# Sharing the first copies between two engines, and turning one tile of the last chunk, in an attention and feed-forward kernel

## The chip, the cores and the metric

The kernel runs on one core of one Trainium2 chip. The metric is the device time of one execution in microseconds (us); lower is better. A second number, the span, is what the profile of one execution covers; it is about 2 us shorter than the time. The granted clock is the share of TensorE's full speed that the profile records. Times inside an execution are counted from the start of the span.

The engines are TensorE (PE in the profile, with PEld for its weight loads), VectorE (DVE), ScalarE (ACT), GpSimd (POOL) and SyncE (SP). All of them run at once, each through its own queue, and wait for one another by semaphores.

## The reference

```python
# B, H, S, D = 4, 4, 1088, 32;  r = 8;  everything float32
def phi(x):                                   # 32 numbers of a token become 64
    a = np.einsum('rd,bhsd->bhsr', S1, x)
    b = np.einsum('rd,bhsd->bhsr', S2, x)
    return np.einsum('bhsi,bhsj->bhsij', a, b).reshape(*x.shape[:-1], r * r)
q_p, k_p = phi(q), phi(k)
kv  = np.einsum('bhsf,bhsd->bhfd', k_p, v)
z   = np.sum(k_p, axis=2)
num = np.einsum('bhsf,bhfd->bhsd', q_p, kv)
den = np.einsum('bhsf,bhf->bhs', q_p, z)[..., None] + 1e-06
x   = (num / den).transpose(0, 2, 1, 3).reshape(B * S, H * D)   # 4352 tokens of 128
h   = np.maximum(x @ w_in, 0.0)                                 # d_ff = 2048
out = h * h @ w_out
```

## The kernel before

The feed-forward part is nearly all of the work, and TensorE is its limit. A batch has 1088 tokens, cut into three chunks of 384, 384 and 320 tokens. `w_in` and `w_out` are cut into 16 blocks of the inner dimension. So there are 4 x 3 x 16 = 192 blocks; each is one product with `w_in` (`pg`), a squared ReLU (`gt`, `g2`) on ScalarE and VectorE, and one product with `w_out` that adds into `po`. The attention of the next batch is planned into the gaps of the running one. Only batch 0's attention has nothing to hide behind: this is the prologue. And only the last chunk's result has nothing behind it: this is the tail. The change touches these two ends.

What the prologue does, in order: products `kf` of the keys with `S1` and `S2`; their outer products `kp`; products of `kp` with the values (`kvp`); the queries' features through three matrices held in `sr` (`rep`, `qp`); `nd`, the numerator and denominator; then `den` and a scaling on VectorE, a transpose (`xp`, `xT`), and the first block of the feed-forward part.

```python
WARM0, WARM = 11, 4             # filler products that keep TensorE busy early on
LA = 3                          # the first product runs three blocks ahead of the second
KG = [[(0, 2), (2, 2), (4, 4), (8, 1)]] + ...   # batch 0: key tiles by group (first, count)
fpool = ctx.enter_context(tc.tile_pool(name="ffn", bufs=5))
...
# loads, one SyncE queue in program order (v's tail of 64 rows from ScalarE)
load_qk(kn[0], k, 0, 0, 512);  load_qk(kn[0], k, 0, 512, S)
load_qk(qn[0], q, 0, 0, 384)
load_v(vn[0], 0, 0);  load_v(vn[0], 0, 2, (nc.scalar, nc.scalar));  load_v(vn[0], 0, 1)
for c in range(2):
    nc.sync.dma_start(w_in32[:, 1024*c : 1024*c + 1024], moe_w_in[:, 1024*c : 1024*c + 1024])
load_qk(qn[0], q, 0, 384, S)                    # the rest of q, behind w_in
...                                             # w_out
# GpSimd's queue: 12 copies for sr, 4 for sq, the identity, and later v's tail
for h in range(H):
    for j_, o_, f_ in ((2, ...), (0, ...), (1, ...)):
        nc.gpsimd.tensor_copy(_ap(sr, 32*h, 32, 128*j_ + 32*h, ...), _ap(s_T, 0, 32, o_, f_))
for h in range(H):
    nc.gpsimd.tensor_copy(sq[32*h : 32*h + 32, 32*h : 32*h + 16], s_T[:, 0:16])
iden = cpool.tile([128, 128], F32);  make_identity(nc, iden[:])
...
# the prologue in program order (each engine takes its own in this order)
keep_warm(WARM0)
... # kf, fs for the four groups
replicated(2, 0, 128, psf, "pg")                # rep, first 128 columns
a_v(0, 0, nc.scalar)                            # v's first half, copied by ScalarE
a_kp(0, 0);  a_kv0(0);  a_kp(0, 1)
a_kv(0, 0);  a_kv(0, 1)                         # kvp, tiles 0 and 1
replicated(0, 0, 128, ...);  replicated(1, 0, 128, ...)
a_fs(0, 2);  a_fs(0, 3)
a_v(0, 1, nc.scalar)                            # v's second half
a_v(0, 2, nc.gpsimd)                            # v's tail: last in GpSimd's queue
a_kp(0, 2);  a_kp(0, 3)
for t in range(2, 9):
    a_kv(0, t)                                  # kvp, the other seven tiles
...
replicated(2, 128, 384, ...); ...               # rep, the other 256 columns
a_kvz(0)
for c in range(2):
    nc.scalar.copy(w_in[:, 1024*c : ...], w_in32[:, 1024*c : ...])   # float32 to float16
for t in range(3):
    a_nd(0, t)
...
# the main loop and the tail
for i in range(NS + 4):                         # NS = 192
    if i + LA < NS:
        ffn1(i + LA, act_square(i + LA))
    if 0 < i < NS:
        ffn2(i)                                 # w_o is stationary, g2 moves
    ...                                         # the work planned for this block
f_last(B - 1, 2)

def f_last(b, ch):                              # the three tiles of the last chunk
    po = st["po", b, ch]                        # columns are tokens
    for i in range(3):
        ...
        # copy a tile out of PSUM, turn it with TensorE, scale it by beta per token, store it
        (nc.vector.tensor_copy if i == 1 else nc.scalar.copy)(oT[:, 0:w], po[:, 128*i : 128*i + w])
        nc.tensor.transpose(op[0:w, 0:128], oT[:, 0:w], iden[:, :])
        ...                                     # scaling: VectorE for i == 1, ScalarE otherwise
        (nc.sync, nc.gpsimd, nc.scalar)[i].dma_start(
            bass.AP(out.tensor, out.offset + (b*S + 4*t) * 128,
                    [[128, w // 32], [G * 128, 32], [1, 128]]),     # 4 x 32 rows of 512 bytes
            ob[0:w, :])
```

## Time and profile before

| | before |
|---|---|
| time, median of the 3 runs given | 206.92 us (206.01 to 207.1) |
| span of the profiled run | 204.8 us, granted clock 0.997 |
| TensorE busy | 96% of the span |
| `den` starts (VectorE, end of the prologue's products) | 15.33 us |
| first feed-forward block starts | 18.16 us |
| block 8 starts | 24.41 us |
| block 176 (last before the last chunk) starts | 184.28 us |
| block 176 to the end of the span | 20.49 us |

The profile's page gives the busy times (with the share of the span and the number of instructions), the busy tenths of 40 equal slices, and the shares of the chain that ended last:

```profile
span 204.8 us, 3685 instructions
PE 196.1 (96%) x1180; PEld 124.2 (61%) x1180; DVE 143.1 (70%) x387; ACT 143.8 (70%) x322; POOL 60.4 (30%) x254
...
PE   7998999999999999999999999999999999999980
...
PE 65%; issue 21%; POOL 5%; DVE 4%; DMA 1%; ACT 1%; POOLq 0%; ACTq 0%; DVEq 0%
```

TensorE's row is nearly full from the first slices (of 5.1 us each) on, but its filler products count as busy too, so the row doesn't show the prologue's waits; the chain does. GpSimd's 5% of the chain is the surprise: an engine that is idle 70% of the time holds up the end. The chain of waits in order of time says where (start, us, what):

```profile
6.92 2.50 POOL sr L228 x3
...
9.48 0.27 POOL sq L233
...
11.43 0.24 POOL va_119 L253
...
11.71 0.42 PE kvp L321 x8
12.13 1.49 PE rep L612 x6
...
13.70 1.60 PE nd L390 x12
15.33 0.18 DVE den L406
```

Up to 11.67 us the chain is GpSimd's queue: copies for `sr`, then `sq`, the identity, and last the small copy of v's tail (`va`), for which TensorE waits.

The view by tile gives the minimum, median and maximum of those copies in ns, and the timeline (start, us, engine, line, operation, output from input, count, and in brackets the idle time before it and its releaser) shows what VectorE did meanwhile. First the tile view of `sr` in before, then the timeline of before:

```profile
L228 POOL COPY sr<-s_T x12: 201/204/1217, 5.3 to 8.2; 32x32 f32<-32x32 f32 x12
```

```profile
5.28 4.14 POOL L228 COPY sr<-s_T 32x32 f32<-32x32 f32 x12
...
7.53 2.17 DVE L301 TENSOR_TENSOR kp<-fs 128x512 f32<-128x512 f32 x3
...
11.71 0.42 PE L321 MATMUL kvp<-kp,va_119 128*33 128x64 f32 x8 [0.29 <-POOL va_119 L253]
...
18.16 0.22 PE L491 MATMUL pg<-xT,w_in 128*128 128x128 f16 x1
...
22.15 1.43 DVE L379 TENSOR_TENSOR qp<-qa,qb 128x384 f32<-128x384 f32 x2
...
22.47 1.59 POOL L248 COPY va_122<-vn 128x512 f32<-128x512 f32 x2 [0.27 <-POOL br L529]
```

The tail in the timeline of before:

```profile
197.27 0.70 PE L513 MATMUL po<-g_2684,w_o 128*128 128x320 f32 x2
198.01 0.27 ACT L570 COPY oTl<-po 128x128 f32<-128x128 f32 x1 [1.72 <-PE po L513]
...
199.09 0.71 SPq L582 DMA_DIRECT2D out_dram<-obl  x1
...
199.67 0.82 POOL L582 DMA_DIRECT2D out_dram<-obl  x1 [39.43 <-DVE obl L573]
199.94 0.64 ACTq L582 DMA_DIRECT2D out_dram<-obl  x1
```

The last feed-forward product ends at 197.97, and 6.80 us later the span ends. The trace's records of the DMA packets show the three stores landing at 201.33 (SyncE's), 202.71 (GpSimd's) and 203.38 us (ScalarE's). For a store, I call the end of its last packet the landing.

### The profile page before, as it was taken

The numbers are of one execution on the slowest core, as the hardware profiler recorded it, in microseconds if no ns is written. First come the engines' busy times: TensorE is split into PE (matmuls) and PEld (weight loads), VectorE is DVE, ScalarE is ACT, GpSimd is POOL, SyncE is SP. The second block draws the span as 40 slices with busy tenths as digits, with TensorE's granted clock in tenths as the row PEclk, the third lists the DMA queues.
The fourth block names the chain that finished last, engine by engine and source line by source line (L and its number), as shares of the span: only waits on it lengthen the run. The fifth ranks groups of instructions, "written<-read, shape, count | busy, mean of one in ns | idle before, by whom it ended". The sixth has DMA issues, their size and how long they took to land.

```text
span 204.8 us, 3685 instructions
## 1 busy us (share of the span) xinstructions
PE 196.1 (96%) x1180; PEld 124.2 (61%) x1180; DVE 143.1 (70%) x387; ACT 143.8 (70%) x322; POOL 60.4 (30%) x254
## 2 busy tenths in 40 slices
PE   7998999999999999999999999999999999999980
PEld 2774675577657655767576655767576655555640
DVE  3956977895587777976757788776757766667740
ACT  2545979858796877686887777686887765766640
POOL 4934637010426830011826420011826200000001
PEclk9999999999999999999999999999999999999998
DMA  6699401020012563020104840020112010200201
GB/s 187 160 348 239 136 20 22 2 39 0 19 20 38 158 147 77 3 38 2 40 12 71 212 126 0 3 40 0 38 20 41 2 32 0 34 7 0 38 0 32
DMA packets 31305, 12.32 MB, mean 60 GB/s; under 512 B 23399, under 2 KB 29863, under 8 KB 31287
## 3 DMA queue, kind: packets, MB, share of 16 engines
q1 hardware_dynamic: 30820, 11.97, 24.2%
q8 instruction: 9, 0.15, 0.3%
q10 hardware_dynamic: 386, 0.07, 0.2%
q14 instruction: 10, 0.07, 0.2%
q0 software_dynamic: 80, 0.07, 0.1%
HBM read 8.78 MB, written 2.23 MB: 54 GB/s over the span
## 4 chain that ended last, share of the span: by engine, by line
PE 65%; issue 21%; POOL 5%; DVE 4%; DMA 1%; ACT 1%; POOLq 0%; ACTq 0%; DVEq 0%
PE po L513 38%; PE pg L491 10%; PE nd L390 8%; PE kvp L321 3%; PE qc L364 3%; POOL br L529 2%; POOL sr L228 2%; PE kf L275 2%; DMA s_nat<-in_S_dram 1%; PE rep L612 1%; DVE qp L379 1%; ACT gt L500 1%; DVE xs L447 1%; DVE qa L374 1%; DVE mx L411 0%
## 5 line engine op out<-in xcount | busy, mean ns | idle before, releaser
L500 ACT ACTIVATE gt<-pg 128x384 f32<-128x384 f32 (+2 forms) x193 | 89.1, 464 | 39.2 <-PE pg L491 38.3
L491 PE MATMUL pg<-xT,w_in 128*128 128x384 f16 (+2 forms) x193 | 61.0, 316 | 0.5 <-ACT xT L472 0.3
L529 POOL COPY br<-beta 32x3 f32<-32x3 f32 x192 | 43.2, 225 | 50.9 <-DVE beta L454 43.3
L491 PEld LDWEIGHTS <-w_in 128*128 128x128 f16 x193 | 18.9, 98 | 19.9 <-issue 1.2
L582 POOL DMA_DIRECT2D out_dram<-obl x1 | 0.8, 816 | 39.4 <-DVE obl L573 39.4
L374 DVE STREAM_SHUFFLE qa<-qc 128x384 f32<-128x384 f32 x22 | 12.0, 590 | 0.1
L390 PEld LDWEIGHTS nd<-kvz_127,qp 128*128 128x128 f32 x72 | 10.0, 190 | 3.0 <-DVE qp L379 0.2
L379 DVE TENSOR_TENSOR qp<-qa,qb 128x384 f32<-128x384 f32 x22 | 11.7, 567 | 0.1
L390 PEld LDWEIGHTS nd<-kvz_125,qp 128*128 128x128 f32 x72 | 9.8, 190 | 3.2 <-issue 0.5
L537 DVE STREAM_TRANSPOSE oT<-po 128x384 f32<-128x384 f32 (+1 forms) x11 | 6.2, 564 | 7.9 <-PE po L513 7.9
L301 DVE TENSOR_TENSOR kp<-fs 128x1024 f32<-128x1024 f32 (+3 forms) x10 | 10.8, 1109 | 0.3 <-ACT fs L289 0.3
L390 PE MATMUL nd<-kvz_125,qp 128*128 128x132 f32 x72 | 10.2, 278 | 0.2
L390 PE MATMUL nd<-kvz_127,qp 128*128 128x132 f32 x72 | 10.3, 277 | 0.0
L350 POOL COPY kvz_127<-kvt 32x2 f32<-32x2 f32 x8 | 1.5, 186 | 25.8 <-PE pg L491 16.3
L364 PE MATMUL qc<-qT,sq 128*128 128x384 f32 x22 | 8.8, 487 | 0.0
L447 DVE TENSOR_TENSOR xs<-nd,sc 128x384 f16<-128x384 f32 (+2 forms) x13 | 6.7, 522 | 0.3
L595 PE MATMUL warm<-zero 128*128 128x512 f16 x15 | 5.7, 550 | 1.2 <-DVE zero L142 1.2
L259 DVE STREAM_TRANSPOSE qT<-qn 128x1088 f32<-128x1088 f32 (+2 forms) x5 | 5.3, 1057 | 1.9 <-DMA qn<-in_q_dram 1.9
L406 DVE TENSOR_SCALAR den<-nd 128x12 f32<-128x12 f32 x12 | 2.0, 170 | 6.3 <-PE nd L390 6.3
L369 DVE STREAM_SHUFFLE qb<-qc 128x384 f32<-128x384 f32 x11 | 6.4, 586 | 0.0
L411 DVE TENSOR_REDUCE mx<-nd 128x12 f32<-128x384 f32 x12 | 5.9, 495 | 0.0
L543 DVE TENSOR_TENSOR ob<-oT,br 128x384 f32<-128x384 f32 (+1 forms) x11 | 5.9, 534 | 0.0
(677 smaller groups left out, 413.0 us busy)
## 6 DMA issues: line engine op xcount, KB each, us to landing
vn<-in_v_dram SPq DMA_DIRECT2D x32, 64.0 KB, 3.6
kn<-in_k_dram SPq DMA_DIRECT2D x3, 544.0 KB, 7.5
qn<-in_q_dram SPq DMA_DIRECT2D x3, 544.0 KB, 3.6
out_dram<-ob SPq DMA_DIRECT2D x32, 48.0 KB, 1.8
w_in_99<-in_moe_w_in_dram SPq DMA_DIRECT2D x2, 512.0 KB
w_o<-in_moe_w_out_dram SPq DMA_DIRECT2D x2, 512.0 KB, 9.3
out_dram<-ob SPq DMA_DIRECT2D x12, 40.0 KB, 1.9
qn<-in_q_dram SPq DMA_DIRECT2D x1, 352.0 KB
```

Of the source, the lines that this page charges most:

```text
L301: nc.vector.tensor_tensor(out=_ap(kp, 0, 128, 0, [[64, 4 * n], [8, 8], [1, 8]]), in0=_ap(fs, 0, 128, 0, [[8, 4 * n], [1, 8], [0, 8]]), in1 ...
L364: nc.tensor.matmul(qc[:, 0:384], sq[:, :], qT[:, 384 * ch : 384 * ch + 384])
L369: nc.vector.stream_shuffle(in_=st[b, "qc", ch][:, 0:384], out=qb[:, :], mask=mask_b)
L374: nc.vector.stream_shuffle(in_=st[b, "qc", ch][:, 0:384], out=qa[:, :], mask=mask_a[e])
L379: nc.vector.tensor_tensor(out=qp[:, :], in0=st[b, "qa", ch, e][:, :], in1=st[b, "qb", ch][:, :], op=mult)
L390: nc.tensor.matmul(nd[:, 132 * o : 132 * o + 132], st[b, "qp", ch, e][:, 128 * o : 128 * o + 128], st[b, "kvz"][:, 132 * e : 132 * e + 132 ...
L447: nc.vector.tensor_tensor(out=_ap(st[b, "xs", ch], 0, 128, 128 * o, [[32, 4 * n], [1, 32]]), in0=_ap(st[b, "nd", ch], 0, 128, 132 * o, [[3 ...
L491: nc.tensor.matmul(pg[:, c0:c1], w_in[:, 128 * c : 128 * c + 128], st[b, "xT"][:, 384 * ch + c0 : 384 * ch + c1],)
L500: nc.scalar.activation(gt[:, c0:c1], pg[:, c0:c1], Relu)
L513: nc.tensor.matmul(st["po", b, ch][:, c0:c1], w_o[:, 128 * c : 128 * c + 128], g2s[i][1][:, c0:c1], start=(c == 0 and c0 == 0), stop=(c == ...
L529: nc.gpsimd.tensor_copy(_ap(st[b, "br"], 32 * dm, 32, 12 * ch + p0, [[4, 3]]), st[b, "beta"][32 * p0 : 32 * p0 + 32, 3 * ch : 3 * ch + 3],)
L537: nc.vector.transpose(oT[:, 0:n], st["po", b, ch][:, 0:n])
```

## The change

The intent has two halves.

- Prologue: ScalarE, idle at that time, takes four of the twelve `sr` copies, and v's tail moves ahead of `sq` and the identity in GpSimd's queue. The rest of q is loaded ahead of `w_in`. The last two groups of key tiles are cut more evenly, and four `kvp` tiles instead of two are placed early; v's second half is copied in two pieces, the `kvz` copies are dealt out anew, and two filler products go.
- Tail: in the last chunk, the first tile's 128 tokens are kept out of `po`. Their second product is turned around: `g2` is stationary and `w_o` moves, so that the tokens come out on the partitions and need no copy and no transpose. It runs four blocks behind. So the other two tiles finish first, and their copies, transposes and scalings hide under the four late products; only one scaling and one store are left at the end. GpSimd issues no store any more.

```diff
-    WARM0, WARM = 11, 4
+    WARM0, WARM = 10, 3
+    LAST = 4
-    KG = [[(0, 2), (2, 2), (4, 4), (8, 1)]] + [[(0, 4), (4, 5)]] * (B - 1)
+    KG = [[(0, 2), (2, 2), (4, 2), (6, 3)]] + [[(0, 4), (4, 5)]] * (B - 1)
     load_v(vn[0], 0, 1)
+    load_qk(qn[0], q, 0, 384, S)
     ...                                    # the two loads of w_in
-    load_qk(qn[0], q, 0, 384, S)
-    for h in range(H):
-        for j_, o_, f_ in ((2, 8, [[0, 4], [1, 8]]), (0, 0, [[1, 4], [0, 8]]), (1, 4, [[1, 4], [0, 8]])):
-            nc.gpsimd.tensor_copy(
+    for j_, o_, f_, copy in (
+        (2, 8, [[0, 4], [1, 8]], nc.gpsimd.tensor_copy),
+        (1, 4, [[1, 4], [0, 8]], nc.scalar.copy),
+        (0, 0, [[1, 4], [0, 8]], nc.gpsimd.tensor_copy),
+    ):
+        for h in range(H):
+            copy(
                 _ap(sr, 32 * h, 32, 128 * j_ + 32 * h, [[8, 4], [1, 8]]),
                 _ap(s_T, 0, 32, o_, f_),
             )
     ...                                    # sq and the identity: moved down, see below
-    a_kv(0, 0)
-    a_kv(0, 1)
+    for t in range(4):
+        a_kv(0, t)
     ...
-    a_v(0, 1, nc.scalar)
     a_v(0, 2, nc.gpsimd)
+    ...                                    # sq and the identity, now behind v's tail
+    a_v(0, 1, nc.scalar, 0, 2)
     a_kp(0, 2)
+    a_v(0, 1, nc.scalar, 2, 2)
     a_kp(0, 3)
-    for t in range(2, 9):
+    for t in range(4, 9):
         a_kv(0, t)
     ...                                    # kvp's memset earlier, kvz copies dealt out anew
-        if 0 < i < NS:
+        if 0 < i < NS - NFF:
             ffn2(i)
+        elif NS - NFF <= i < NS:           # the last chunk's 16 blocks
+            ffn2_rest(i)                   # columns 128 to 319 into po
+            if i >= NS - NFF + LAST:
+                ffn2_tile(i - LAST)
-    f_last(B - 1, 2)
+    last_copy(B - 1)                       # two copies
+    for i in range(NS - LAST, NS):
+        if i == NS - 2:
+            last_turn(B - 1)               # two transposes, two scalings, two stores
+        ffn2_tile(i)
+    last_tile(B - 1)                       # one scaling, one store (SyncE)
+    def ffn2_tile(i):
+        ...
+        nc.tensor.matmul(st["pt"][:, 0:128], g2s[i][1][:, 0:128],
+                         w_o[:, 128 * c : 128 * c + 128],
+                         start=(c == 0), stop=(c == NFF - 1))
```

Three more buffers of `g2` (eight instead of five) hold what the late tile still needs.

## The prediction

> What bounds the kernel now. The page gives a span of 204.8 us with TensorE (PE) busy 96%, clock 0.997. From about 20 to 198 us the chain of waits is PE work back to back: a feed-forward block takes 0.81 us of PE at 384 columns, 0.67 us at 320. Only the two ends can give time.
>
> Prologue before (chain of waits, timeline). GpSimd works in one queue from 4.8 to 11.67 us: 12 copies into sr (5.28 to 9.42, 0.345 us each), four into sq (0.97), the identity (0.9), last the v tail copy. PE waits for that copy (kvp at 11.71), then does the 256-column rep products to 13.62 and nd to 15.30; VectorE starts den at 15.33.
>
> Prologue after. GpSimd has 8 sr copies, then the v tail (done about 8.4). ScalarE, idle until 6.32, takes four at about 0.2 us each. Next limit: v's second half lands at about 8.3 us (DMA packets by size), ScalarE copies it after fs, and the kp products on VectorE end at about 9.5. The last kvp then ends at about 10.3 instead of 12.13; rep at 11.9 (13.62), nd at 13.4 (15.30). Gain 1.9 us (estimate from these durations). The q rest landed at about 13.2; behind the weights it would have held the earlier chain. The first w_in half now lands near 12, the second near 13.3: the casts (1.04 us each) end near 14.5, before xT (about 16.3) needs them. The dropped fillers end 0.43 us sooner. The Trainium skill, "TensorE: Matmul & The Clock Gate", Part 1, puts clock warm-up at about 3.4 us of activity; ten fillers at 0.43 us still cover it.
>
> Tail before. The last FFN product ends at 197.97; copies, transposes, scalings follow, last issue at 199.94. GpSimd's store delays ScalarE's: their packets interleave, the last landing about 203.4, 3.4 us after its issue started, where SyncE's took about 2.3.
>
> Tail after. Columns per block are the same (192 + 128 = 320); the extra weight loads hide (nd's matmuls of 132 columns, a weight load each, run at 0.112 us). The first four blocks of the last chunk need 0.45 us of PE, not 0.67, but VectorE has oT (0.56) and ob (0.55) there, so PE stalls some 0.4 us. The rest part ends about 0.5 us sooner; its transposes and scalings hide under the four late tile products. PE ends about 1.0 us later than before, but only a 0.35 us scaling and one store remain: last issue at about 199.5 on the old clock, landing 2.5 us later. Gain about 1.65 us. The Trainium skill, "DMA: Bandwidth & Descriptors", Anatomy of one DMA, gives a fixed DMA cost of about 2 us; the trace agrees (ob stores 1.8 to 1.9), so the last store stays exposed.
>
> Sum: 3.6 us; 206.9 to 203.3 us, range 202.2 to 204.6. Faster by over 2%: 0.30; within 2%: 0.68; slower: 0.02.
>
> Signs. Right: last prologue kvp near 10.3, den near 13.4; a PE stall of a few tenths at the fifth block of the last chunk; last issue by SyncE. Wrong: casts or first FFN blocks waiting for DMA; block period in the last chunk above 0.70 us; ScalarE's sr copies delaying fs; last landing over 3 us after its issue.
>
> What would make it wrong: weights landing later; no VectorE-bound stall and a quicker last landing (then over 4.1 us, faster by 2%); or SyncE's two stores queueing by 0.7 us.

## More of the kernel before

A tile's 128 tokens are rows 4t to 4t+3 of each of 32 stretches of 34 tokens, so a store's outermost dimension in device memory is 4 long (2 for the last tile, which has 64 tokens).

I number the products `pg` by their start in the timeline, from 0, and call number n block n. Block 0 makes two of them, so my numbers run one ahead of the kernel's own from there on: "block 8" is its eighth block, and "block 176" is the last one before the last chunk. All runs are counted alike, so the differences don't depend on this. These marks cut the execution into pieces that can be compared one by one.

## The result, and the profile after

| | before | after |
|---|---|---|
| time, median (4 runs each) | 206.81 us (206.01 to 207.1) | 204.22 us (203.67 to 204.56) |
| ratio | | 0.9878, 95% interval 0.9843 to 0.9914 |
| span and clock of the profiled run | 204.8, 0.997 | 202.5, 0.999 |
| `den` starts | 15.33 | 13.89 |
| first block starts | 18.16 | 17.42 |
| block 8 starts | 24.41 | 23.15 |
| block 176 starts | 184.28 | 183.02 |
| block 176 to the end | 20.49 | 19.46 |

A ratio is the mean time of one kernel's fast runs over that of the other's of the same rounds, so it is not quite the ratio of the medians. The change is faster by 1.2%, which counts as "within 2%".

The sum closes. The lead over before is 1.26 us at block 8 and still 1.26 at block 176; the tail adds 20.49 − 19.46 = 1.03. Together that is 2.29, the difference of the two spans (204.77 and 202.48). The prologue's 1.26 is itself a sum: `den` comes 1.44 us sooner, the stretch from `den` to the first block takes 3.53 us instead of 2.83, which gives 0.70 back, and the stretch from there to block 8 takes 5.73 instead of 6.25, which gains 0.52.

The page of after, with the lines that answer to those shown of before:

```profile
span 202.5 us, 3743 instructions
PE 194.5 (96%) x1209; PEld 127.0 (63%) x1209; DVE 143.0 (71%) x388; ACT 144.1 (71%) x325; POOL 58.2 (29%) x249
...
PE 87%; DMA 6%; ACT 2%; SPq 1%; issue 1%; DVE 0%; ACTq 0%
```

GpSimd is gone from the chain. In its place stands DMA with 6%, of which the page gives 4% to the load of `w_in` and 2% to that of v. The tile view of `sr` after shows both engines' copies:

```profile
L240 POOL COPY sr<-s_T x8: 199/204/574, 5.2 to 7.6; 32x32 f32<-32x32 f32 x8
...
L240 ACT COPY sr<-s_T x4: 214/215/216, 4.6 to 5.3; 32x32 f32<-32x32 f32 x4
```

The timeline of after, prologue:

```profile
7.88 0.28 POOL L257 COPY va_119<-vn 64x128 f32<-64x128 f32 x1
...
8.74 0.72 ACT L252 COPY va_119<-vn 128x256 f32<-128x256 f32 x2 [0.54 <-DMA vn<-in_v_dram]
...
9.41 1.31 PE L320 MATMUL kvp<-kp,va_119 128*33 128x64 f32 x40
...
13.89 0.17 DVE L405 TENSOR_SCALAR den<-nd 128x12 f32<-128x12 f32 x1 [0.22 <-PE nd L389]
...
16.15 1.04 ACT L687 CAST w_in<-w_in_100 128x1024 f16<-128x1024 f32 x1 [2.56 <-DMA w_in_100<-in_moe_w_in_dram]
...
17.11 0.53 ACT L471 COPY xT<-xp 128x128 f16<-128x128 f16 x2
```

v's tail is copied at 7.88 instead of 11.43. From `kvp` at 9.41 to the end of `nd`, TensorE works in one row: it is now the prologue's limit, with v's landing before it. Then comes the 0.70 us given back. The second cast of `w_in` waited for its load until 16.15. It keeps ScalarE busy until the end of that cast at 17.19, and the copy `xT` behind it in the queue, without which the first block cannot begin, starts at 17.11 only (the two overlap by a little).

The tail of after:

```profile
187.55 0.30 PE L490 MATMUL pg<-xT,w_in 128*128 128x320 f16 x1
...
188.28 0.30 PE L490 MATMUL pg<-xT,w_in 128*128 128x320 f16 x1
...
196.97 0.39 PE L530 MATMUL pt<-w_o,g_2692 128*128 128x128 f32 x2
197.21 0.65 ACTq L575 DMA_DIRECT2D out_dram<-obl  x1
197.32 1.42 SPq L575 DMA_DIRECT2D out_dram<-obl  x2
197.40 0.35 DVE L610 TENSOR_SCALAR obl<-pt,beta 128x128 f32<-128x128 f32 x1
```

The last product (`pt`) ends 14.34 us after block 176 started, against 13.69 for before's last `po` product. But only 5.12 us follow it, against 6.80. The two 128x320 products at the head of this fence are issued in the fourth and fifth step of the chunk (a first product runs three blocks ahead, so they belong to its seventh and eighth block). They are 0.73 us apart, where the two pairs before are 0.46 us apart: a stall of 0.27 us at the place that the prediction named.

SyncE's second store is the last one. Its data were ready at 197.75, but SyncE was still issuing the 64-row store (0.71 us from 197.32) until 198.03; the store began at 198.14 and the trace's last packet of it, at 201.13, lies 2.99 us behind. Its semaphore is complete at 201.46.

### The profile page after: what moved, and what is told of

Same layout as the page of the kernel before. It is cut to its first block, busy times and chain, and to the rows that moved or that the text cites. A ratio compares the mean times of both kernels' runs of the same rounds, so it can differ in the third digit from the quotient of the medians.

```text
span 202.5 us, 3743 instructions
## 1 busy us (share of the span) xinstructions
PE 194.5 (96%) x1209; PEld 127.0 (63%) x1209; DVE 143.0 (71%) x388; ACT 144.1 (71%) x325; POOL 58.2 (29%) x249
## 4 chain that ended last, share of the span: by engine, by line
PE 87%; DMA 6%; ACT 2%; SPq 1%; issue 1%; DVE 0%; ACTq 0%
PE po L513 55%; PE pg L490 15%; PE nd L389 7%; DMA w_in_100<-in_moe_w_in_dram 4%; PE kvp L320 3%; PE qc L363 3%; DMA vn<-in_v_dram 2%; PE pt L530 2%; PE kf L279 2%; ACT gt L499 2%; SPq L104 1%; ACT w_in L687 1%; SPq L114 0%; ACT xT L471 0%; SPq L160 0%
## 5 line engine op out<-in xcount | busy, mean ns | idle before, releaser
L545 POOL COPY br<-beta 32x3 f32<-32x3 f32 x192 | 42.6, 222 | 50.1 <-DVE beta L453 42.5
L305 DVE TENSOR_TENSOR kp<-fs 128x512 f32<-128x512 f32 (+3 forms) x10 | 10.8, 1108 | 0.5 <-ACT fs L293 0.4
L389 PE MATMUL nd<-kvz_127,qp 128*128 128x132 f32 x72 | 10.3, 277 | 0.0
L363 PEld LDWEIGHTS qc<-qT,sq 128*128 128x128 f32 x22 | 4.1, 190 | 2.7
L621 PE MATMUL warm<-zero 128*128 128x512 f16 x13 | 4.6, 516 | 1.2 <-DVE zero L143 1.2
```

Of the source, the lines that this page charges most:

```text
L305: nc.vector.tensor_tensor(out=_ap(kp, 0, 128, 0, [[64, 4 * n], [8, 8], [1, 8]]), in0=_ap(fs, 0, 128, 0, [[8, 4 * n], [1, 8], [0, 8]]), in1 ...
L363: nc.tensor.matmul(qc[:, 0:384], sq[:, :], qT[:, 384 * ch : 384 * ch + 384])
L389: nc.tensor.matmul(nd[:, 132 * o : 132 * o + 132], st[b, "qp", ch, e][:, 128 * o : 128 * o + 128], st[b, "kvz"][:, 132 * e : 132 * e + 132 ...
L545: nc.gpsimd.tensor_copy(_ap(st[b, "br"], 32 * dm, 32, 12 * ch + p0, [[4, 3]]), st[b, "beta"][32 * p0 : 32 * p0 + 32, 3 * ch : 3 * ch + 3],)
```

## The experiments

Twelve kernels ran, all with a correct result. Kernels on one chip share its runs of before: the first four; the next four; then `e9_changed_again`, `e10_stores_split` and `e11_last_two`; and last `e12_before_v_later` alone. The medians of before were 206.65, 207.44, 206.57 and 207.18 us.

### Are the two ends independent?

`e1_prologue_only` is the changed kernel with before's tail (`ffn2` for all blocks, `f_last`, five `g2` buffers). `e2_tail_only` is before with the new tail alone.

```diff
 e1: main loop and tail as before
-        if 0 < i < NS - NFF:
+        if 0 < i < NS:
             ffn2(i)
-        elif NS - NFF <= i < NS: ...
-    last_copy(B - 1) ... last_tile(B - 1)
+    f_last(B - 1, 2)
 e2: the same lines the other way round, in before
```

> The changed prologue with the old tail. If the two ends are independent (the middle is TensorE work back to back, and step 8 to step 176 keep one constant shift of 1.26 us in the two traces), this gains 1.26 us of span: about 203.5 us of span, ratio near 0.994; the tail from the last FFN product to the end of the span stays at 6.8 us. Rival: the ends interact (deeper g2 buffers or another schedule help the middle); then the shift at step 176 differs from 1.26 us.

Measured: 205.18 us median, ratio 0.9904 [0.9857, 0.995]. `den` at 14.29, block 8 at 22.99 (1.42 us ahead of before), and the tail takes 20.51 us, as before.

> The old prologue with the changed tail. If the ends are independent, step 176 starts at 184.3 us as in the kernel before, and the whole gain is 1.0 us in the tail: span about 203.7, ratio near 0.995. The first four blocks of the last chunk stall TensorE by about 0.2 to 0.4 us at the fifth, and the last store of SyncE lands about 3.1 us after its issue started, because its packets share DMA engines with the 64-row store issued just before. If the prologue matters for the tail, the sum of the two gains differs from the 2.3 us of both by over 0.3 us.

Measured: 205.53 us, ratio 0.9927 [0.9879, 0.9976]. Block 176 starts at 184.23, as before, and the tail takes 19.52 us, 0.97 less.

What follows: each half keeps its gain without the other. 1.0% and 0.7% add up to 1.7%, against 1.2% for both in the first comparison and 1.35% in a later one (`e9_changed_again`); the intervals are wide enough for both to be the same sum. The profiles are the sharper tool here: the prologue's gain is 1.3 to 1.4 us and the tail's 1.0 us.

### Was it the late cast that gave 0.7 us back?

Theory: the second cast of `w_in` stands in front of `xT` in ScalarE's queue. If GpSimd makes it, the stretch from `den` to the first block returns to 2.83 us.

```diff
-    for c in range(2):
-        nc.scalar.copy(w_in[:, 1024*c : 1024*c + 1024], w_in32[:, 1024*c : 1024*c + 1024])
+    nc.scalar.copy(w_in[:, 0:1024], w_in32[:, 0:1024])
     ...
+    nc.gpsimd.tensor_copy(w_in[:, 1024:2048], w_in32[:, 1024:2048])
     f_br(0, 0)
```

> The changed kernel, but the second half of the w_in cast is done by GpSimd instead of ScalarE. My theory: ScalarE waits 2.6 us for the late second half of w_in (landed at 16.1 us) with the xT copy queued behind it, so that the first FFN block is only 0.74 us earlier than before, though den is 1.44 us earlier. Then here the first FFN block starts near 16.7 us instead of 17.4, and the steady shift at step 8 grows from 1.26 to between 1.4 and 1.5 us; span down by 0.1 to 0.3 us against the changed kernel. Rival: the late cast costs nothing, as the early blocks have slack to take it up: then the first block starts earlier but step 8 is where it was, 23.15 us.

Measured: 205.11 us, ratio 0.9903 [0.9852, 0.9955], no gain. The timeline of this run, and the clock row of its page:

```profile
14.98 1.04 POOL L706 CAST w_in<-w_in 128x1024 f16<-128x1024 f32 x1 [2.97 <-DMA w_in<-in_moe_w_in_dram]
...
15.34 0.71 DVE L426 TENSOR_SCALAR mp<-mm 128x3 f32<-128x3 f32 x1
...
18.93 1.48 PE L513 MATMUL po<-g,w_o 128*128 128x128 f32 x4
```

```profile
PEclk9998899999999999999999999999999999999999
```

The expectation failed for two reasons, neither of which I had foreseen. First, VectorE's tiny `mp`, 3 numbers per partition, took 0.71 us instead of 0.17 and ended at 16.05, just behind GpSimd's cast at 16.02. The Trainium skill, "SBUF — State Buffer", section "Who interferes with whom", says that the two engines share a pair of ports as an exclusive lock, that some VectorE instructions, `tensor_scalar` among them, can take it, and that "the other **fully blocks**". The trace agrees: `mp` ended with the cast, not in proportion to anything. So from `den` to the first block still took 3.37 us. Second, from 18.64 to 22.05 us the trace's clock record gives TensorE half its rate: the four `po` products took 1.48 us here, where the same four take 1.00 in after. Block 8 came at 24.61. Two of the six runs had such a lower clock (0.989 and 0.990, against 0.997 to 1.0). The late cast's cost is therefore not settled by this run. The repeat below settles it another way.

### Does the place of q's load matter?

```diff
     load_v(vn[0], 0, 1)
-    load_qk(qn[0], q, 0, 384, S)
     ...                                  # the two loads of w_in
+    load_qk(qn[0], q, 0, 384, S)
```

> The changed kernel with one part undone: the rest of q is loaded behind w_in again. The prediction said that q would then hold the chain: q lands at about 13.2 us, qT takes 0.9 us, so den starts near 14.3 instead of 13.9 us and the shift falls by about 0.4 us. Rival: the reordering is what made the second half of w_in late, so that undoing it frees ScalarE (second cast done near 14.5 us) and the first FFN block starts near 17.0 us, earlier than the 17.4 of the changed kernel, with step 8 no later than 23.15 us.

Measured: 204.83 us, ratio 0.988 [0.9833, 0.9928], span 202.5: the same as the changed kernel. The timeline of this run:

```profile
13.52 0.91 DVE L263 STREAM_TRANSPOSE qT<-qn 128x704 f32<-128x704 f32 x1 [0.35 <-DMA qn<-in_q_dram]
...
14.36 0.13 DVE L405 TENSOR_SCALAR den<-nd 128x12 f32<-128x12 f32 x1
```

The rest of q landed at 13.08 instead of 9.53. VectorE waited for it, and the transpose, from 13.52 to 14.43, stands in front of `den` in VectorE's queue. So `den` came 3.32 us after the last `kvp`, where it is 3.17 in every other changed prologue, and block 8 came at 23.05, 12.02 us after that `kvp`, where e1, e5 and e7 to e11 have 11.87. The prediction's sentence that q behind the weights would have held the faster chain is thus right in kind, but the hold is 0.15 us and not 0.4. The rival is right in its first half: with q behind it, the last of `w_in` landed at 12.21 and the second cast ended at 14.40; with q ahead of it, the last of `w_in` landed between 13.90 and 15.73 in all ten profiles. The two effects are small and work against each other, and the times don't tell the two orders apart.

### Does the prologue wait for v?

In after, ScalarE waits 0.54 us for v's second half. `e5_v_issued_first` issues v's tail after the second half instead of before it.

```diff
     load_v(vn[0], 0, 0)
-    load_v(vn[0], 0, 2, (nc.scalar, nc.scalar))
     load_v(vn[0], 0, 1)
+    load_v(vn[0], 0, 2, (nc.scalar, nc.scalar))
```

> The changed kernel, with the two small v tail loads issued after the eight large v loads, so that the second half of v waits for two transfers fewer. Theory: what holds the changed prologue is when v lands (ScalarE waited 0.45 and 0.54 us for its two halves, and the last kvp ended at 10.7 us, not at the predicted 10.3). Then the second va copy starts before 8.5 us instead of 8.74, the last kvp ends near 10.3 to 10.5 us and den starts near 13.6 us instead of 13.9. Rival: v is not what holds it (kp on VectorE or the ScalarE copies are); then the last kvp stays at 10.7 us or later.

Measured: 204.18 us, ratio 0.9865 [0.9828, 0.9902]. ScalarE's copy began at 8.72 (8.74 in after), the last `kvp` ended at 11.34 and `den` came at 14.51, later than in after. The theory is not supported, but the run is confounded: five of the 18 `kf` passes (two for each of nine products) took 0.21 us here instead of the 0.11 of after.

That difference turned out to be a rule. Over the ten profiles in which the `sr` copies are shared, `den` comes the later, the more `kf` passes ran at half rate:

| `kf` passes at half rate | runs | `den` starts |
|---|---|---|
| 0 | after, e3, e9, e10 | 13.89 to 14.05 |
| 1 | e7 | 14.14 |
| 2 or 3 | e4, e8, e1 | 14.23 to 14.36 |
| 5 | e5 | 14.51 |
| 6 | e11 | 14.62 |

With before's prologue (before, e2, e12; eleven fillers) no pass ran at half rate; the changed prologue has ten, starts `kf` 0.2 to 0.6 us sooner, and is on TensorE's chain. The trace's clock record puts the rise to the full clock at 4.24 us in after, at 5.42 to 5.54 in the three profiles with before's prologue, and as late as 6.91 in e11. The Trainium skill, "TensorE: Matmul & The Clock Gate", Part 1, says that the clock is raised by a free-running window of activity, so that the moment varies from run to run. The runs agree: the same program had 0 half-rate passes in two profiles (after, e9), and kernels with the same prologue instructions had 1 to 6 (e7, e8, e1, e11). The first profile of after happened to be a lucky one on this count. (In e4, 0.15 us of `den`'s 14.36 is the wait for q.)

The same profiles bound what v can cost. From the start of the last `kf` pass to the end of the last `kvp` it is 3.45 us in seven of the ten, `e5_v_issued_first` among them, and 3.56 to 3.67 in the three with the earliest `kf` (after, e3, e10). So v's landing cost after some 0.17 us (3.62 − 3.45, an estimate), and nothing where the clock rose later.

### What did sharing the `sr` copies give?

```diff
-        (1, 4, [[1, 4], [0, 8]], nc.scalar.copy),
+        (1, 4, [[1, 4], [0, 8]], nc.gpsimd.tensor_copy),
```

> The changed kernel with one part undone: all 12 sr copies on GpSimd again (the v tail copy still ahead of sq and the identity). If taking copies off GpSimd is what pays, the last sr copy ends near 9.2 us instead of 7.8, the two small rep products start near 9.2 instead of 8.8, the last kvp near 11.2 instead of 10.7, and den is 0.4 to 0.5 us later than 13.9. Rival: moving the v tail ahead of sq and the identity is all that pays, and sharing with ScalarE is worth nothing: den within 0.1 us of 13.9.

Measured: 205.47 us, ratio 0.9923 [0.9879, 0.9967], span 203.8. The timeline of this run, and its tile view of `sr`:

```profile
5.37 4.75 POOL L240 COPY sr<-s_T 32x32 f32<-32x32 f32 x12
...
10.17 0.71 PE L638 MATMUL rep<-qT,sr 128*128 128x128 f32 x4 [0.96 <-POOL sr L240]
```

```profile
L240 POOL COPY sr<-s_T x12: 199/204/839, 5.4 to 9.9; 32x32 f32<-32x32 f32 x12
```

The copies end at 10.12, the small `rep` products wait for them, the last `kvp` ends at 12.12 and `den` comes at 15.29: before's 15.33 to within 0.04. Everything else of the change's prologue is in this kernel, and none of it pays without this one line. (Whether the line would pay without the rest was not run.) I had expected about a third of that, because I priced a copy at its mean. The tile views give the reason. A copy's median is 0.20 us in all three kernels, but the ones that meet VectorE's `kp` products (two operands in SBUF) last as long as those do: up to 1.22 us in before, 0.84 here, 0.57 in after. In before, nine copies took 1.64 us (5.28 to 6.92), and the last three 2.50. So the four copies that ScalarE takes are worth more than four times 0.2 us: GpSimd's last `sr` copy ends at 7.82 in after and at 10.12 here, and of the last four copies here, from 8.16 on, two met `kp`. That the lock causes it is my reading of the durations with the skill's section on ports; no run took `kp` away from the copies.

### The tail: where do the last 5 us go?

Three kernels try to shorten the landing of the stores. `e7_small_store_scalar` moves the 64-row store from SyncE to ScalarE, so that SyncE is free for the last one.

```diff
-            store(b, t, ob, w, nc.scalar if i == 1 else nc.sync)
+            store(b, t, ob, w, nc.scalar)
```

> The changed kernel with the 64-row store issued by ScalarE after its own store, so that SyncE has only the last store to issue. In the changed kernel SyncE's issue of the last store had to wait from 197.75 to 198.14 us for its issue of the 64-row store. If queueing on SyncE is what makes the end late, the last store's issue starts 0.3 us sooner after the scaling and the span falls by about 0.3 us. Rival: the packets of both stores meet on the same DMA engines whoever issues them; then the last landing moves by under 0.1 us.

Measured: 204.16 us, ratio 0.986 [0.982, 0.99]. The last store is issued at 197.74, as soon as its data are ready, and lands at 200.34. But now the 64-row store is issued second by ScalarE, at 197.95, and lands at 201.11. The tail takes 19.40 us, against 19.46. SyncE's queueing is not the limit; whichever store starts last ends about 3 us later.

`e8_store_16_engines` asks why a store takes so long. In the trace, a 128-row store ends with 4 completion packets and a 64-row store with 2. The Trainium skill, "DMA: Bandwidth & Descriptors", section "Why a DMA increments its semaphore by 16 and not by 1", says that a transfer is dealt to the largest number of DMA engines, at most 16, that divides the outermost dimension of both sides, and always to the lowest-numbered ones. The outermost dimension of this store is 4. So four engines carry 32 rows of 512 bytes each, at about 27 ns a packet in the trace, and the other stores use the same engines. This experiment puts the tile's tokens in another order from the first product on, so that the outermost dimension becomes 32.

```diff
+        if (b, ch) == (B - 1, 2):                # the first product of the last chunk, in two parts
+            nc.tensor.matmul(pg[:, 0:128], w_in[...],
+                             _ap(st[b, "xT"], 0, 128, 768, [[1, 32], [32, 4]]))
+            c0 = 128                             # the rest: columns 128 to 319
-        store(b, 6, ob, 128, nc.sync)
+        nc.sync.dma_start(bass.AP(out.tensor, out.offset + (b * S + 24) * 128,
+                                  [[G * 128, 32], [128, 4], [1, 128]]), ob[:, :])
     ...                                          # beta reordered by four small DMAs; 64 rows on ScalarE
```

> As the run with the small store on ScalarE, and the last tile's tokens reordered (four to a row block) so that its store has 32 row blocks instead of 4 and is spread over 16 DMA engines. Each FFN product of the last chunk is split in two for it. If the 32 packets per engine, 0.9 us, and the meeting with the 64-row store set the last landing, it comes about 0.8 us sooner after its issue than the 3.0 us of the changed kernel, and the span falls by 0.6 to 1.0 us, less what the split products cost (at most 0.3 us). If the landing is a fixed cost, it falls by under 0.2 us.

Measured: 206.29 us, ratio 0.9963 [0.9925, 1.0], and the time says nothing about the store: the split products cost far more than the 0.3 us that I allowed (the last product ends 17.15 us after block 176, not 14.34). Within the profile the store itself is clear. It ends with 16 completion packets and lands 1.87 us after its issue began, where the 4-engine store took 2.99. The last landing was then the 64-row store's, on two engines.

`e10_stores_split` gets the same without reordering anything: one DMA per 32 rows, so that the outermost dimension is 32 on both sides.

```diff
-    def store(b, t, ob, w, eng):
-        eng.dma_start(bass.AP(..., out.offset + (b * S + 4 * t) * 128,
-                              [[128, w // 32], [G * 128, 32], [1, 128]]), ob[0:w, :])
+    def store(b, t, ob, w, *engs):
+        for p0, eng in enumerate(engs):
+            eng.dma_start(bass.AP(..., out.offset + (b * S + 4 * t + p0) * 128,
+                                  [[G * 128, 32], [1, 128]]), ob[32 * p0 : 32 * p0 + 32, :])
     # 64-row store: SyncE, ScalarE; last store: SyncE three times, ScalarE once
```

> The changed kernel with the 64-row store as two DMAs of 32 rows and the last store as four, given to SyncE and ScalarE. Each then has 32 row blocks outermost and goes over 16 DMA engines, as the store in the sixteen-engine run did (landed 1.9 us after its issue), without that run's split products. If the landing is set by 32 packets in line on the few engines that both stores share, the last issue starts at about 1.3 us after TensorE's last product (0.5 us later than now, being the third in line) and lands 1.9 us later instead of 3.0: the time from the last product to the end of the span falls from 5.1 to about 4.6 us. If a landing costs 2.5 us or more whatever its shape, that time grows to 5.2 us or more.

Measured: 203.51 us (202.96 to 203.76), ratio 0.984 [0.9802, 0.9877], the fastest of all (`e9_changed_again` took 203.93). The timeline of its tail:

```profile
196.67 0.66 ACTq L585 DMA_DIRECT2D out_dram<-obl  x1
196.78 1.81 SPq L576 DMA_DIRECT2D out_dram<-obl  x4
196.85 0.35 DVE L623 TENSOR_SCALAR obl<-pt,beta 128x128 f32<-128x128 f32 x1
197.43 0.89 ACTq L576 DMA_DIRECT2D out_dram<-obl  x2
```

The tile view of `out_dram` from 195 us on, which takes the semaphore for the landing (of the stores on 16 engines):

```profile
DMA to landing us min/median/max: 1.4/2.0/2.2
```

Two more issues make SyncE's queue longer; its last one starts at 198.18. But each of these DMAs now has 16 completion packets, and the last landing is at 199.33, 1.15 us after that. From the end of the scaling to the last landing it is 2.13 us (197.20 to 199.33), against 3.38 in after (197.75 to 201.13). From the last product to the end of the span it is 4.34 us, against 5.12, and the whole tail takes 18.68 us, against 19.46.

The end gains only 0.78 us where the last packet gains 1.25, because the kernel waits for the semaphore. By the trace's semaphore records the last store's is complete at 200.18 here, 2.00 us after the issue and 0.85 us after the last packet. In after it is complete at 201.46, 3.32 us after the issue and 0.33 us after the last packet. From the end of the scaling to the complete semaphore it is thus 2.98 us against 3.71, a gain of 0.73. Both stores were cut at once; which cut pays how much was not separated.

### The changed kernel again, and four blocks or two

`e9_changed_again` is the changed kernel without an edit.

> The changed kernel once more, unaltered. The profiles so far say that the end of the prologue moves from run to run with when the w_in halves land and when TensorE's clock doubles (18 kf passes are 0.11 us apart, but the first ones 0.21 in most runs), so the step 8 start should lie between 22.8 and 23.3 us and the second w_in cast start anywhere from 14.5 to 16.2 us. Rival: the late cast (16.15 us) belongs to this load order; then it is again after 15.9 us.

Measured: 203.93 us (203.72 to 204.71), ratio 0.9865 [0.983, 0.99]. The timeline of this run:

```profile
14.78 1.04 ACT L687 CAST w_in<-w_in 128x1024 f16<-128x1024 f32 x1 [1.27 <-DMA w_in<-in_moe_w_in_dram]
...
16.54 0.76 ACT L471 COPY xT<-xp 128x128 f16<-128x128 f16 x2 [0.72 <-PE xp L462]
```

Here the cast starts at 14.78 and ends at 15.82, and `xT` waits for TensorE's transpose instead. The stretch from `den` to the first block is 2.83 us, and block 8 comes at 22.73, not 23.15. In eight other profiles with this ScalarE cast (e1, e4, e5, e6, e7, e8, e10, e11), it starts between 13.36 and 15.18, and the stretch is 2.83 us in all of them but e4 (2.96). So the 0.70 us came of one very late landing of `w_in`'s second half (15.73 us). What belongs to the change is a smaller delay: with the rest of q ahead of it, this half landed at 13.90 to 14.77 us in nine other profiles, against 12.18 to 12.56 in the four with q behind it (before, e2, e4, e12). In the ScalarE runs among the nine the cast still ended before `xT` needed ScalarE. Priced by the other runs' pieces, that profile would have had block 8 at 13.89 + 2.83 + 5.87 = 22.59; it lost 0.56 us. Why this landing was so late I cannot say: the other runs with the same order of loads did not have it.

`e11_last_two` holds the tile back two blocks instead of four.

```diff
-    LAST = 4
+    LAST = 2
```

> The changed kernel with the tile kept two blocks behind instead of four. Theory: of the 0.85 us of TensorE work put off, 0.27 us was lost to a stall at the fourth and fifth block, as ScalarE and VectorE cannot feed blocks of 0.45 us while they also do oT and ob. With two blocks put off the stall is at most 0.1 us, but TensorE then waits 0.3 us at the end for the oTl copies ahead of the transposes; the time from step 176 to the last product is within 0.2 us of the 14.3 us of the changed kernel, and the span within 0.3 us. If there were no stall with four, two would be 0.3 us slower.

Measured: 204.23 us, ratio 0.9875 [0.984, 0.991]. The stall at the fifth block is gone (the blocks go from 0.46 to 0.68 us without one), but TensorE waits 0.3 us for the copy before the transposes, and the last product ends 14.52 us after block 176 instead of 14.34. The tail takes 19.67 us, 0.2 more. The stall of 0.27 us is the smaller evil.

### Where did 0.4 us between the first block and block 8 come from?

In after and e4 the stretch takes 5.73 us, in seven other changed prologues 5.87, and in before, e2 and e6 6.25 (e3 ran at half clock there). The 0.14 us between 5.73 and 5.87 make good part of a late first block: in e4, 2.96 + 5.73 us is the same as 2.83 + 5.87 elsewhere, to 0.01. The rest, 0.38 us, is the question here. Nothing in the change is meant to act there. Before's timeline shows one `qp` product of VectorE that took 0.97 us instead of 0.54 while GpSimd copied v for batch 1 (22.47, shown above); in e6, whose prologue ends as late as before's, it took 0.98 us. In after, those copies start at 22.90, behind the pair of `qp` products that ran at 21.27. `e12_before_v_later` is before with only the earliest step of these copies moved, by six; the kernel's planner then puts them behind the `br` copies, 13.2 us later.

```diff
-            P.add(("v", n, part), "POOL", 1.0, [], a_v, n, part, nc.gpsimd, first=s0 + 6)
+            P.add(("v", n, part), "POOL", 1.0, [], a_v, n, part, nc.gpsimd, first=s0 + (12 if n == 1 else 6))
```

> The kernel before, with GpSimd's copies of the second batch's v put after its br copies, later by some 20 blocks. In the kernel before, the first FFN block starts at 18.16 us and block 8 at 24.41, 6.25 us apart; in most changed kernels 5.87. There a qp product on VectorE took 0.97 us instead of 0.54 while GpSimd copied v beside it, and the nd products of TensorE waited for that product. If this overlap is the cause, block 8 here follows block 0 by 5.8 to 5.9 us, block 8 starts near 24.0 us, and the span falls by 0.3 to 0.4 us. If it is not, the two are again 6.25 us apart. The v copies may cost time later, when the second batch needs them; the start of block 48 against block 8 (42.33 us before) shows it.

The timeline of this run:

```profile
22.34 1.01 DVE L379 TENSOR_TENSOR qp<-qa,qb 128x384 f32<-128x384 f32 x2
...
35.67 1.51 POOL L248 COPY va<-vn 128x512 f32<-128x512 f32 x2
```

Measured: the two `qp` products take 1.01 us together, against 1.43, and the stretch is 5.87 us. The cause is shown: the meeting of the two engines cost before 0.38 us, and the shift of the prologue happened to pull them apart. No later stretch pays for it (block 8 to block 48 takes 42.34 us, 42.33 in before). In after, a later pair of `qp` products meets the moved copies and takes 1.43 us, but the stretch from block 8 to block 48 is 42.33 there too: the same conflict costs nothing where VectorE has slack. The time does not show it: 206.3 us, ratio 0.9979 [0.9877, 1.0081], no clear difference, since `den` happened to come 0.18 us later in this run and one run had a clock of 0.989.

## Why the prediction was right or wrong

The prediction was 203.3 us, within 202.2 to 204.6; the kernel took 204.22. The class and the range hold, the mechanism holds, and the size was too large: 3.6 us were promised, and 2.3 us of span and 2.6 us of median time came.

| step | predicted | measured in the profile of after |
|---|---|---|
| four `sr` copies on ScalarE | about 0.2 us each | 0.215 us each: right |
| v's tail copied | done about 8.4 | 8.16: right |
| last `kvp` of the prologue | near 10.3 | 10.72 |
| `den` | near 13.4 | 13.89 (14.6 at worst in other runs) |
| casts of `w_in` end | near 14.5 | 17.19, in `e9_changed_again` 15.82 |
| gain of the prologue | 1.9 | 1.26 (1.09 to 1.80 in other profiles) |
| stall at the fifth block of the last chunk | a few tenths | 0.27 us: right |
| TensorE's end, against before | about 1.0 later | 0.65 later |
| last issue, on the old clock | about 199.5, by SyncE | 198.14 + 1.26 = 199.40, by SyncE: right |
| last landing after its issue | 2.5 | 2.99 |
| gain of the tail | about 1.65 | 1.03 |

**The prologue's term was mis-sized.** The direction is right and its cause is shown by `e6_sr_on_gpsimd`. Three things stand between 1.9 and 1.26. `den` came 1.44 us sooner and not 1.9, because the last `kvp` ended 0.4 us later than I had it. The `kp` products ended at 9.58, close to the forecast 9.5, but the 40 passes of the last five `kvp` tiles began only at 9.41 and took 1.31 us, where I had left 0.8 us after `kp`; v's late landing is about 0.17 us of this (estimate above). The late cast took 0.70, of which the next stretch gave 0.14 back: 0.56 net. The other 0.38 of that stretch's 0.52 is the conflict that `e12_before_v_later` isolates; the prediction did not have that gain at all, so it is luck that it makes up for part of the late cast.

**A sign against the prediction came true, and was cheap by luck.** "Casts or first FFN blocks waiting for DMA" was to show that it was wrong. The second cast waited for its load in all nine profiles that have it on ScalarE with q ahead (0.29 to 2.56 us): the forecast of "near 13.3" for the second half of `w_in` was 0.6 us or more too early in every one. Only in after did the wait reach the first block.

**The tail's term failed in two steps.** "The last issue at about 199.5" was right to 0.1 us. "Landing 2.5 us later" was wrong: 2.99, since the store runs on four engines that it shares with the two stores just before it. And the arithmetic was loose. From before's last landing at 203.4, an issue at 199.5 plus 2.5 gives a gain of 1.4, not the 1.65 that I wrote. With 2.99, the same sum gives 1.0, which is what was measured. The prediction named "last landing over 3 us after its issue" as a sign against it, and 2.99 came as near to that as can be.

**"Ten fillers still cover it" was half right.** Of the 18 `kf` passes, 0 to 6 ran at half rate from run to run, and `den` moved by 0.7 us with them. In the three profiles with before's prologue no pass was at half rate, and GpSimd's queue was longer anyway.

**"The q rest behind the weights would have held the earlier chain" was right, but small**: 0.15 us in `e4_q_behind_weights`, where I expected 0.4.

**The mean of an `sr` copy hid what it was made of.** 0.345 us each was right as a mean, and the end of GpSimd's queue was forecast well. But 0.20 us of work and the rest waiting is another thing than 0.345 us of work: it led me to expect too little in `e6_sr_on_gpsimd`.

**That weight loads and columns would cost nothing was right.** The period of the last chunk's blocks is 0.68 us, against 0.67.

What stays open: why `w_in`'s second half landed at 15.73 us in one of the profiles with that order of loads; why some executions of before ran at a clock of about 0.988 and took 2 us longer (the half clock of `e3_cast_gpsimd` lasted 3.41 us, which costs up to 1.7 us by my estimate and would fit, but no profile of before caught one); and whether an earlier v would help where the clock rises early, since the one run that tried it had the half-rate passes against it.

## What to carry to other kernels

When a long-running kernel is full in the middle, mark three or four fixed points in the timeline and compare the pieces between them: a gain of one per cent that drowns in the spread of whole runs can be read to 0.1 us this way, and each piece has its own cause. Before pricing a queue of small copies by its mean, look at the minimum and maximum: a copy that takes six times its median is waiting, and taking copies off such a queue can be worth more than their own time (2.3 us for four copies of 0.2 us here). For the last store of a kernel, count its completion packets: cutting it so that its outermost dimension is a multiple of 16 brought the time from ready data to the last packet from 3.38 to 2.13 us here, and to the complete semaphore, which is what the kernel waits for, from 3.71 to 2.98, although it took four more issues.

## What the Trainium skill lacked or had wrong

- "TensorE: Matmul & The Clock Gate", HAM oscillation, gives the rule that TensorE must have no idle gap over about 3.4 us, and the section after it names a second mode with frequent short gaps, without a number. In `e3_cast_gpsimd` TensorE fell to half rate from 18.64 to 22.05 us although no gap around there was over 0.74 us. The 3.41 us before the fall held 2.07 us of TensorE work (61%). In after the 3.41 us from 14.48 to 17.90 held 2.39 us (70%), and no fall came. The pages have no figure for how sparse is too sparse; these are one case each.
- "DMA: Bandwidth & Descriptors", Anatomy of one DMA, gives a fixed cost of about 2.0 us, measured on the path through GpSimd, and no separate figure for stores issued by SyncE. A store of 32 rows issued by SyncE had its semaphore complete 2.00 us after its issue began, and its last packet after 1.15 us (`e10_stores_split`).
- The same page tells how many engines a transfer gets, and the trace agrees (2, 4 and 16 completion packets), but not what few engines cost at the end of a kernel: with 4 engines the last packet of the last store came after 2.99 us, with 16 after 1.87 (`e8_store_16_engines`), or 1.15 cut into four. To the complete semaphore it is 3.32, 2.20 and 2.00 us.
- No page has a figure for how much the landing of a load of half a megabyte varies among other loads: in ten profiles with q's rest ahead of it, `w_in`'s second half landed between 13.90 and 15.73 us; in four with q behind it, between 12.18 and 12.56.
